# Two kv heads per 2 MB tile, on even and odd partitions, in a KV-cache decode layer

## Chip, cores and metric

The kernel runs on one core of a Trainium2 chip. The metric is the device time of one execution in microseconds (us). The median of the kernel before was 404.53 us over four runs (404.59 us over the three known when the prediction was made).

## The reference

It is one decode step of a layer with 4 sequences. Attention with 32 query heads and 16 kv heads looks at the last 4096 positions of a cache; then comes a gated feed-forward block.

```python
q = (layernorm(x) @ wq)                       # 4 x 32 heads x 128
k = k_cache[:, :, Sk - 4096:, :]              # 4 x 16 x 4096 x 128, bf16; V alike
p = softmax(einsum(q, k) * 128 ** -0.5)       # two query heads share a kv head
h = x + einsum(p, v) @ wo
g, u = layernorm(h) @ W_gate, layernorm(h) @ W_up      # 576 x 4608 each
out = h + (relu(g) * u) @ W_down
```

K and V of the window are 64 + 64 blocks of 1 MB (134.2 MB), and all weights together are 25.4 MB. Every byte is read once. The window of one head is 1 MB of contiguous memory; two neighbouring heads lie 4 MB apart.

## The kernel before

One DMA brings the 1 MB of one head and batch: partition p gets positions 32p to 32p+31, a contiguous run of 8 KB. K is transposed on TensorE (PE) in 32 blocks of 128 positions, copied from PSUM to SBUF, and multiplied with q. The scores of all 16 heads of a batch collect in two PSUM banks. P is then exponentiated, transposed, and multiplied with V. The sync engine (SP) issues all large loads in one order into a ring of 16 slots; it waits until the last reader of a slot is done.

```python
NSLOT = 16                     # slots of TILE = 4096 bf16 per partition = 1 MB
def add_kv(kind, i):
    b, kvh = divmod(i, KVH)
    s = ring_slot()
    off = slot0 + s * TILE
    src = (A_k_cache if kind == "K" else A_v_cache)[b, kvh, SK - WIN:SK, :].rearrange("(p t) d -> p (t d)", p=128)
    place((kind, i), off, TILE, ("TR", i) if kind == "K" else ("PV", i),
          lambda e: e.dma_start(out=arena[:, off:off + TILE], in_=src), key=f"slot{s}")
# ... (cut)
# QK: one head per tile, 512 neighbouring columns
    bank[4 + u][32 * j:32 * j + 32, :], lhsT=qTm[:, b, kvh, :],
    rhs=k[:, j * 1024 + u * 512:j * 1024 + (u + 1) * 512],
# exp of a batch, 1024 columns; then eight transposes of P and two copies into pTm
    act(("EXP", b), lambda e: e.activation(out=p_sb[:, :], in_=s_ps, func=ACT.Exp, ..., accum_out=stat[:, b, 2:3]), ...)
```

## Time and profile before

| quantity | value | where it is read |
|---|---|---|
| time | 404.5 us | median of the runs |
| DMA rate while K and V stream | 419 GB/s | windows of the profile |
| PE, DVE, ACT busy over the span | 66, 30, 34% | part 1 of the page |
| a K tile from issue to landing | 27.9 us | part 6 of the page |
| last W_down landed, end of span | 398.3, 402.3 us | chain of waits |

The first fence is from the page of the kernel before. In part 2 each column is a fortieth of the span: the digit is the busy share in tenths, then follow the GB/s moved. Part 6 gives the size of a DMA and the median time from issue to landing.

```profile
span 402.3 us, 10840 instructions
...
PE 265.4 (66%) x5091; PEld 209.7 (52%) x5091; DVE 121.9 (30%) x218; ACT 138.3 (34%) x154; POOL 3.9 (1%) x21
...
DMA  8999999999999999999999999999999999999992
GB/s 321 372 402 422 419 419 419 419 418 421 419 418 421 419 420 419 421 419 418 419 420 419 420 419 420 416 421 419 421 419 419 412 367 370 425 422 415 209 360 118
DMA packets 25172, 160.29 MB, mean 398 GB/s; under 512 B 2404, under 2 KB 6504, under 8 KB 6504
...
sb_arena<-in_A_k_cache_dram SPq DMA_DIRECT2D x64, 1024.0 KB, 27.9
```

The DMA engines are busy in every slice, and from slice 4 to slice 31 the rate hardly moves. A tile that needs 2.5 us of transfer lands 28 us after it was issued, so a long queue stands in front of the engines; 27.9 us at 419 GB/s is 11.7 MB. No compute engine is full. The kernel is bound by bytes per second of the DMA engines.

The second fence is the window view of the same kernel: start and end in us, length, busy us of PE, PE weight loads, DVE, ACT and POOL with instruction counts, granted clock, DMA share, GB/s.

```profile
87.00:200.00 113.00, 84.03 (x1637) 69.27 (x1636) 37.08 (x63) 45.89 (x49) 0.00 (x0) 0.86 1.01 419
200.00:320.00 120.00, 84.50 (x1777) 69.39 (x1776) 35.27 (x64) 42.59 (x47) 0.00 (x0) 0.81 1.01 419
```

The third is the end of its chain of waits (start us, us, what): the chain runs into the last W_down transfer, then 4 us of work.

```profile
335.17 18.48 DMA sb_arena<-in_A_v_cache_dram
...
359.93 38.40 DMA sb_arena<-in_B_W_down_dram
398.33 0.04 issue
398.38 1.30 PE psb L593 x32
```

The groups that the change touches in its arithmetic are the exp (L416), one of the two copies of the transposed P (L437), and QK (L402). They are four, four and 512 instructions (busy us, mean ns).

```profile
L402 PE MATMUL psb<-sb_arena,sb_qTm 128*32 128x512 bf16 x512 | 44.0, 425 | 1.0 <-ACT sb_p_sb L416 1.0
L437 DVE COPY sb_pTm<-psb 128x512 bf16<-128x512 bf16 x4 | 2.4, 593 | 3.6 <-PE psb L425 3.6
L416 ACT ACTIVATE sb_p_sb<-psb,sb_stat 128x1024 bf16<-128x1024 f32 x4 | 4.5, 1114 | 6.2 <-DVE sb_stat L412 6.2
```

### The profile page before, as it was taken

What the parts mean: (1) busy time and instruction counts of PE and PEld (TensorE: products, weight loads), DVE (VectorE), ACT (ScalarE), POOL (GpSimd) and SP (SyncE); (2) the same over time, 40 slices, a digit from 0 to 9 for tenths busy, and PEclk for the clock granted to TensorE, in tenths of its full rate; (3) what the DMA queues carried; (4) which work ended last, traced back from release to release, by engine and by line L of the source; (5) the groups of instructions that cost most, each with busy time, mean ns of one, the idle gap of its engine ahead of it and who ended that gap; (6) DMA issues with size and microseconds to landing.
All of it is one profiled execution on the core that took longest, in us unless ns stands there. A gap on an engine that the chain in (4) does not pass through costs nothing.

```text
span 402.3 us, 10840 instructions
## 1 busy us (share of the span) xinstructions
PE 265.4 (66%) x5091; PEld 209.7 (52%) x5091; DVE 121.9 (30%) x218; ACT 138.3 (34%) x154; POOL 3.9 (1%) x21
## 2 busy tenths in 40 slices
PE   4555999988777776867776767877774420465253
PEld 4244777766566655656564656666653320342022
DVE  4147555643222243422222433322232000011020
ACT  4222777754333353434333532533330100000010
POOL 3000000000000000000000000000000000000000
PEclk9866999999888889888889897988886555566556
DMA  8999999999999999999999999999999999999992
GB/s 321 372 402 422 419 419 419 419 418 421 419 418 421 419 420 419 421 419 418 419 420 419 420 419 420 416 421 419 421 419 419 412 367 370 425 422 415 209 360 118
DMA packets 25172, 160.29 MB, mean 398 GB/s; under 512 B 2404, under 2 KB 6504, under 8 KB 6504
## 3 DMA queue, kind: packets, MB, share of 16 engines
q1 hardware_dynamic: 25104, 159.59, 98.2%
q8 instruction: 40, 0.66, 0.7%
q10 hardware_dynamic: 24, 0.01, 0.0%
q14 instruction: 4, 0.03, 0.0%
HBM read 159.58 MB, written 0.00 MB: 397 GB/s over the span
## 4 chain that ended last, share of the span: by engine, by line
DMA 67%; PE 19%; SPq 9%; DVE 3%; issue 1%; ACT 0%
DMA sb_arena<-in_A_k_cache_dram 42%; PE psb L373 13%; DMA sb_arena<-in_A_v_cache_dram 11%; DMA sb_arena<-in_B_W_down_dram 10%; SPq L225 8%; DMA sb_arena<-in_A_wq_dram 4%; PE psb L402 3%; DVE sb_pTm L496 2%; PE psb L452 1%; PE psb L518 1%; SPq L232 1%; PE psb L593 0%; DVE sb_stat L410 0%; ACT sb_p_sb L416 0%; PE psb L331 0%
## 5 line engine op out<-in xcount | busy, mean ns | idle before, releaser
L373 PE MATMUL psb<-sb_ident_b,sb_arena 128*128 128x128 bf16 x2048 | 151.9, 243 | 60.4 <-DMA sb_arena<-in_A_k_cache_dram 53.8
L373 PEld LDWEIGHTS psb<-sb_ident_b,sb_arena 128*128 128x128 bf16 x2048 | 140.1, 111 | 74.2 <-DMA sb_arena<-in_A_k_cache_dram 60.2
L387 ACT COPY sb_arena<-psb 128x1024 bf16<-128x1024 bf16 x128 | 125.4, 1014 | 143.2 <-PE psb L373 143.2
L385 DVE COPY sb_arena<-psb 128x1024 bf16<-128x1024 bf16 x128 | 87.9, 690 | 152.0 <-PE psb L373 151.7
L452 PE MATMUL psb<-sb_arena,sb_pTm 128*32 128x128 bf16 x2048 | 49.2, 251 | 32.7 <-DMA sb_arena<-in_A_v_cache_dram 31.5
L452 PEld LDWEIGHTS psb<-sb_arena,sb_pTm 128*32 128x32 bf16 x2048 | 41.6, 113 | 50.7 <-DMA sb_arena<-in_A_v_cache_dram 35.5
L402 PE MATMUL psb<-sb_arena,sb_qTm 128*32 128x512 bf16 x512 | 44.0, 425 | 1.0 <-ACT sb_p_sb L416 1.0
L560 PE MATMUL psb<-sb_arena,sb_hnT 128*32 128x384 bf16 (+1 forms) x120 | 10.2, 500 | 14.8 <-DMA sb_arena<-in_B_W_up_dram 8.4
L523 ACT COPY sb_pTm<-psb 128x288 f32<-128x288 f32 x1 | 0.4, 398 | 46.4 <-PE psb L518 46.4
L478 DVE COPY sb_o_sb<-psb 128x128 f32<-128x128 f32 x4 | 1.2, 291 | 45.2 <-PE psb L452 45.2
L560 PEld LDWEIGHTS psb<-sb_arena,sb_hnT 128*32 128x32 bf16 (+1 forms) x120 | 4.0, 130 | 20.4 <-DMA sb_arena<-in_B_W_up_dram 10.4
L402 PEld LDWEIGHTS psb<-sb_arena,sb_qTm 128*32 128x32 bf16 x512 | 8.1, 97 | 9.0 <-issue 3.3
L564 ACT ACTIVATE sb_pTm<-psb 128x384 f32<-128x384 f32 x3 | 1.3, 492 | 23.9 <-PE psb L560 23.9
L567 DVE TENSOR_TENSOR sb_pTm<-psb,sb_pTm 128x384 bf16<-128x384 f32 x3 | 1.5, 550 | 24.0 <-ACT sb_pTm L564 24.0
L331 PE MATMUL psb<-sb_arena,sb_xnT 128*32 128x512 bf16 (+1 forms) x40 | 3.9, 478 | 6.8 <-DMA sb_arena<-in_A_wq_dram 6.4
L496 DVE MEMSET sb_pTm<- 128x8192 uint32 x1 | 6.9, 6885 | 1.6 <-issue 1.6
L593 PE MATMUL psb<-sb_arena,sb_pTm 128*32 128x144 bf16 x144 | 3.9, 277 | 4.2 <-DMA sb_arena<-in_B_W_down_dram 4.2
L416 ACT ACTIVATE sb_p_sb<-psb,sb_stat 128x1024 bf16<-128x1024 f32 x4 | 4.5, 1114 | 6.2 <-DVE sb_stat L412 6.2
L410 DVE TENSOR_REDUCE sb_stat<-psb 128x1 f32<-128x1024 f32 x4 | 4.9, 1225 | 4.3 <-PE psb L402 4.3
L468 ACT ACTIVATE sb_stat<-sb_stat 128x1 f32<-128x1 f32 x4 | 0.8, 203 | 14.5 <-DVE sb_stat L466 14.5
L593 PEld LDWEIGHTS psb<-sb_arena,sb_pTm 128*32 128x32 bf16 x144 | 3.2, 121 | 4.8 <-DMA sb_arena<-in_B_W_down_dram 4.6
L331 PEld LDWEIGHTS psb<-sb_arena,sb_xnT 128*32 128x32 bf16 (+1 forms) x40 | 0.7, 99 | 9.2 <-DMA sb_arena<-in_A_wq_dram 8.7
(94 smaller groups left out, 64.7 us busy)
## 6 DMA issues: line engine op xcount, KB each, us to landing
sb_arena<-in_A_k_cache_dram SPq DMA_DIRECT2D x64, 1024.0 KB, 27.9
sb_arena<-in_A_v_cache_dram SPq DMA_DIRECT2D x64, 1024.0 KB, 27.6
sb_arena<-in_B_W_down_dram SPq DMA_DIRECT2D x4, 1296.0 KB, 36.5
sb_arena<-in_A_wo_dram SPq DMA_DIRECT2D x1, 4608.0 KB, 31.7
sb_arena<-in_B_W_gate_dram SPq DMA_DIRECT2D x4, 1152.0 KB, 27.0
sb_arena<-in_B_W_up_dram SPq DMA_DIRECT2D x4, 1152.0 KB, 28.4
sb_arena<-in_A_wq_dram SPq DMA_DIRECT2D x4, 1024.0 KB, 11.2
sb_arena<-in_B_W_gate_dram SPq DMA_DIRECT2D x1, 576.0 KB, 33.5
```

What stands on the lines that cost most here:

```text
L225: lambda e: e.dma_start(out=arena[:, off:off + TILE], in_=src), key=f"slot{s}")
L331: pe("QMM", lambda e, c=c, w=w, off=off, n=n, g=g, bk=bk: e.matmul(bank[4 + bk][32 * g:32 * g + 32, :], lhsT=xnT[0:w, c, :], rhs=arena[0:w ...
L373: o = pe(("TRJ", i, j), lambda e, j=j, u=u, t=t: e.transpose(out=bankb[TRB[j]][:, u * 128:(u + 1) * 128], in_=kn[:, t, :], identity=ident_ ...
L385: dve(("EV", i, j), lambda e: e.tensor_copy(out=dst, in_=src), deps)
L387: act(("EV", i, j), lambda e: e.copy(out=dst, in_=src), deps)
L402: o = pe(("QK", i), lambda e, u=u, j=j: e.matmul(bank[4 + u][32 * j:32 * j + 32, :], lhsT=qTm[:, b, kvh, :], rhs=k[:, j * 1024 + u * 512:j ...
L410: dve(("MAX", b), lambda e: e.tensor_reduce(out=stat[:, b, 0:1], in_=s_ps, axis=AX.X, op=ALU.max, negate=True), [("QK", b * KVH + KVH - 1)])
L416: act(("EXP", b), lambda e: e.activation(out=p_sb[:, :], in_=s_ps, func=ACT.Exp, bias=stat[:, b, 1:2], scale=SCALE, accum_out=stat[:, b, 2 ...
L452: pe(("PV", i), lambda e, tl=tl, j=j: e.matmul(o_ps[32 * j:32 * j + 32, 0:DH], lhsT=pTm[:, tl, j, kvh, :], rhs=v[:, 8 * j + tl, :], start= ...
L496: dve("c_pTm", lambda e: e.memset(pflat, 0.0))
L560: pe(("GU", c), lambda e, c=c, w=w, g=g, m=m, j=j, lo=lo: e.matmul(bank[3 * g + m][32 * j:32 * j + 32, 0:384], lhsT=hnT[0:w, c, :], rhs=ar ...
L593: pe("DOWN", lambda e, j=j, r=r, n=n, wv=wv: e.matmul(bank[0][32 * n:32 * n + 32, 0:144], lhsT=hhT[:, r * 128 + 32 * j:r * 128 + 32 * j + 32],
```

## The change

Its intent: longer contiguous runs per DMA packet. A run of 16 KB per partition means that 64 partitions hold a whole head, so a 128-partition tile holds two heads. Head 0 goes to the even partitions and head 1 to the odd ones, so that the source can be written with its 64 rows outermost (64 rows x 2 heads x 16 KB). The transposed K then has the two heads in alternate columns, and QK reads every second column. For PV both heads lie in the contraction: each column of P is written twice, transposed, and masked so that one head's weights are zero on odd partitions, the other's on even ones. The sum of exp counts each value twice, so it is multiplied by 0.5. Tiles are 2 MB in a ring of 8 slots. The wq rows are also brought in pairs, 16 KB per partition.

```diff
-NSLOT = 16
-TILE = 4096
-VDMA_LAG = KVH + 2
+NSLOT = 8
+TILE = 8192
+VDMA_LAG = BT + 1
@@ add_kv @@
-            src = (A_k_cache if kind == "K" else A_v_cache)[b, kvh, SK - WIN:SK, :].rearrange("(p t) d -> p (t d)", p=128)
+            src = cache[b, 2 * k2:2 * k2 + 2, SK - WIN:SK, :].rearrange("a (p t) d -> p a (t d)", p=64)
@@ pe_qk @@
-                        rhs=k[:, j * 1024 + u * 512:j * 1024 + (u + 1) * 512],
+                        bank[4 + u][32 * j:32 * j + 32, :], lhsT=qTm[:, b, 2 * k2 + a, :], rhs=k[:, j, :, :, a],
@@ act_exp @@
-            act(("EXP", b), lambda e: e.activation(out=p_sb[:, :], in_=s_ps, func=ACT.Exp, ...
+            act(("EXP", b), lambda e: e.activation(out=p_sb[:, :].rearrange("p (k a) -> p k a", a=2),
+                                                   in_=bass.AP(tensor=psb, offset=4 * 512, ap=[[4096, 128], [1, 1024], [0, 2]]), ...
@@ put_pT, now twice per batch @@
-                    dve(("PM", b, 0), lambda e, dst=dst, src=src: e.tensor_copy(out=dst, in_=src), deps)
+                dve(("PM", b, r, a), lambda e, dst=dst, src=src, a=a: e.tensor_scalar(
+                    out=dst, in0=src, scalar1=par[:, a:a + 1], scalar2=None, op0=ALU.mult), deps)
... (cut: ring bookkeeping, wq in pairs of rows, constants for parity and 0.5; of the old copies only the first is shown)
```

More of the change, by code (lines that the diff above doesn't have):

```diff
@@ L21 @@
 NPAIR = B * KVH
+NTILE = NPAIR // 2
+BT = KVH // 2
 SCALE = DH ** -0.5
@@ L25 @@
 NKT = 3
-NSLOT = 16
-TILE = 4096
+NSLOT = 8
+TILE = 8192
+UNIT = 4096
 QLAG = 2
-VDMA_LAG = KVH + 2
+VDMA_LAG = BT + 1
 PV_LAG = KVH + 3
@@ L144, in bass_sequential_preLN__sliding_block_cached__glu_gated_reglu__decode_kernel @@
         pool = lambda name, fn, deps=(): P.op("gpsimd", name, fn, deps)
-        arena = sb("arena", [128, (NKT + NSLOT) * TILE], BF16)
-        pTm = sb("pTm", [128, 8, 4, KVH, 32], BF16)
+        arena = sb("arena", [128, NKT * UNIT + NSLOT * TILE], BF16)
+        pTm = sb("pTm", [128, 16, 4, BT, 32], BF16)
         ident_b = sb("ident_b", [128, 128], BF16)
@@ L151, in bass_sequential_preLN__sliding_block_cached__glu_gated_reglu__decode_kernel @@
         ones_f = sb("ones_f", [128, 128], FP32)
+        ones_h = sb("ones_h", [128, 128], FP32)
         ones_d = sb("ones_d", [128, 128], FP32)
@@ L163, in bass_sequential_preLN__sliding_block_cached__glu_gated_reglu__decode_kernel @@
         qTm = sb("qTm", [128, B, KVH, 32], BF16)
-        p_sb = sb("p_sb", [128, 1024], BF16)
+        p_sb = sb("p_sb", [128, 2048], BF16)
+        half = sb("half", [128, 64], FP32)
+        par = sb("par", [128, 2], FP32)
         stat = sb("stat", [128, B, 8], FP32)
@@ L182, in bass_sequential_preLN__sliding_block_cached__glu_gated_reglu__decode_kernel @@
         hhT = pflat[:, 4608:4608 + 1152]
-        kT = [arena[:, i * TILE:(i + 1) * TILE] for i in range(NKT)]
-        slot0 = NKT * TILE
+        kT = [arena[:, i * UNIT:(i + 1) * UNIT] for i in range(NKT)]
+        slot0 = NKT * UNIT
         psb = es.enter_context(nc.psum_tensor("psb", [128, 8, 512], FP32))
@@ L210, in place @@
             land[name] = off
-        ring = [(-DC - 2 * NPAIR) % NSLOT]
+        ring = [(-3 - 2 * NTILE) % NSLOT]
         def ring_slot():
@@ L219, in add_kv, with add_wq @@
         def add_kv(kind, i):
-            b, kvh = divmod(i, KVH)
+            b, k2 = divmod(i, BT)
             s = ring_slot()
             off = slot0 + s * TILE
-            src = (A_k_cache if kind == "K" else A_v_cache)[b, kvh, SK - WIN:SK, :].rearrange("(p t) d -> p (t d)", p=128)
-            place((kind, i), off, TILE, ("TR", i) if kind == "K" else ("PV", i),
+            cache = A_k_cache if kind == "K" else A_v_cache
+            src = cache[b, 2 * k2:2 * k2 + 2, SK - WIN:SK, :].rearrange("a (p t) d -> p a (t d)", p=64)
+            place((kind, i), off, TILE, ("TR", 2 * i + 1) if kind == "K" else ("PV", 2 * i + 1),
                   lambda e: e.dma_start(out=arena[:, off:off + TILE], in_=src), key=f"slot{s}")
-        def add_wq(c):
+        wq_off = []
+        def add_wq(m):
             s = ring_slot()
             off = slot0 + s * TILE
-            w = _dw(c)
-            place(("wq", c), off, TILE, "QMM",
-                  lambda e: e.dma_start(out=arena[0:w, off:off + H * DH], in_=A_wq[c * 128:c * 128 + w, :]), key=f"slot{s}")
-        P.dma("scalar", ("L", "x"), lambda e: e.dma_start(out=x_bf[:, :], in_=A_x.rearrange("b s d -> (b s) d")), "d_x")
-        for s in range(2):
-            add_kv("K", s)
-        for c in range(DC):
-            add_wq(c)
-        for s in range(2, NPAIR):
+            if m < 2:
+                wq_off.extend([off, off + H * DH])
+                src = A_wq[m * 256:(m + 1) * 256, :].rearrange("(p r) n -> p (r n)", r=2)
+                place(("wq", m), off, TILE, "QMM", lambda e: e.dma_start(out=arena[:, off:off + TILE], in_=src), key=f"slot{s}")
+            else:
+                wq_off.append(off)
+                place(("wq", m), off, TILE, "QMM",
+                      lambda e: e.dma_start(out=arena[0:64, off:off + H * DH], in_=A_wq[512:576, :]), key=f"slot{s}")
+        P.dma("scalar", ("L", "x"), lambda e: e.dma_start(out=x_bf[:, :], in_=A_x.rearrange("b s d -> (b s) d")), "d_x")
+        add_kv("K", 0)
+        for m in range(3):
+            add_wq(m)
+        for s in range(1, NTILE):
             add_kv("K", s)
@@ L243, in bass_sequential_preLN__sliding_block_cached__glu_gated_reglu__decode_kernel @@
         for i in range(NKT):
-            for blk in range(i * TILE // 64, (i + 1) * TILE // 64):
+            for blk in range(i * UNIT // 64, (i + 1) * UNIT // 64):
                 owner[blk] = "QKEND"
@@ L249, in bass_sequential_preLN__sliding_block_cached__glu_gated_reglu__decode_kernel @@
         WDJ = 9 * D
-        rest = list(range(NPAIR - VDMA_LAG, NPAIR))
+        rest = list(range(NTILE - VDMA_LAG, NTILE))
         for n, v in enumerate(rest):
             add_kv("V", v)
-            if n == len(rest) - 7:
+            if n == len(rest) - 4:
                 place(("wo",), WO_OFF, H * D, "WO",
@@ L273, in kv @@
         def kv(kind, i):
-            off = land[(kind, i)]
+            off = land[(kind, i // 2)]
             return arena[:, off:off + TILE].rearrange("p (t d) -> p t d", d=DH)
@@ L284, in bass_sequential_preLN__sliding_block_cached__glu_gated_reglu__decode_kernel @@
                                                 compare_op=ALU.not_equal, fill=1.0, base=0, channel_multiplier=1), ["c_idf0"])
+        pool("c_half0", lambda e: e.memset(half[:, :], 0.0))
+        pool("c_half", lambda e: e.affine_select(out=half[:, :], in_=half[:, :], pattern=[[-2, 64]], compare_op=ALU.not_equal,
+                                                 fill=1.0, base=0, channel_multiplier=1), ["c_half0"])
+        pool("c_onesh", lambda e: e.memset(ones_h[:, :], 0.5))
         pool("c_ones", lambda e: e.memset(ones_f[:, :], 1.0))
@@ L300, in bass_sequential_preLN__sliding_block_cached__glu_gated_reglu__decode_kernel @@
         dve("c_eps", lambda e: e.memset(eps_c[:, :], EPS))
+        dve("c_par0", lambda e: e.tensor_reduce(out=par[:, 0:1], in_=half[:, :], axis=AX.X, op=ALU.max), ["c_half"])
+        dve("c_par", lambda e: e.tensor_scalar(out=par[:, 1:2], in0=par[:, 0:1], scalar1=-1.0, scalar2=1.0,
+                                               op0=ALU.mult, op1=ALU.add), ["c_par0"])
         dve("c_qTm", lambda e: e.memset(qTm[:, :, :, :], 0.0))
@@ L315, in bass_sequential_preLN__sliding_block_cached__glu_gated_reglu__decode_kernel @@
         tpv = bankb[6]
+        xn_rows = lambda c: (xn_bf[0:B, 512:576] if c == 4 else
+                             xn_bf[0:B, c // 2 * 256:c // 2 * 256 + 256].rearrange("b (p r) -> b r p", r=2)[:, c % 2, :])
         def pe_q():
@@ L319, in pe_q @@
                 w = _dw(c)
-                pe(None, lambda e, c=c, w=w: e.transpose(out=tpv[0:w, c * 4:(c + 1) * 4], in_=xn_bf[0:B, c * 128:c * 128 + w],
+                pe(None, lambda e, c=c, w=w: e.transpose(out=tpv[0:w, c * 4:(c + 1) * 4], in_=xn_rows(c),
                                                          identity=ident_b[0:B, 0:B]), ["xn", "c_idb"] if c == 0 else [])
@@ L327, in pe_q @@
                 w = _dw(c)
-                off = land[("wq", c)]
+                off = wq_off[c]
                 for n in range(8):
@@ L333, in pe_q @@
                         start=(c == 0), stop=(c == DC - 1), skip_group_check=True),
-                        ([("L", "wq", c)] + (["xnT", "c_xnT"] if c == 0 else [])) if n == 0 else [])
+                        ([("L", "wq", c // 2)] + (["xnT", "c_xnT"] if c == 0 else [])) if n == 0 and c % 2 == 0 else [])
             for bk in range(2):
@@ L363, in pe_tr @@
                 for u in range(8):
-                    t = j * 8 + u
+                    t = j * 16 + i % 2 * 8 + u
                     deps = []
                     if u == 0:
-                        deps = [("L", "K", i)] if j == 0 else []
+                        deps = [("L", "K", i // 2)] if j == 0 else []
                         if i == 0:
@@ L389, in pe_qk @@
         def pe_qk(i):
-            b, kvh = divmod(i, KVH)
-            k = kT[i % NKT]
-            for u in range(2):
+            dp, u = divmod(i, 2)
+            b, k2 = divmod(dp, BT)
+            k = kT[i % NKT].rearrange("p (j t k a) -> p j t k a", j=4, t=8, a=2)
+            for a in range(2):
                 for j in range(4):
                     deps = []
-                    if u == 0:
+                    if a == 0:
                         deps.append(("EV", i, j))
-                    if j == 0 and kvh == 0:
+                    if j == 0 and k2 == 0:
                         if b == 0:
@@ L401, in pe_qk @@
                             deps += [("EXP", b - 1), ("MAX", b - 1)]
-                    o = pe(("QK", i), lambda e, u=u, j=j: e.matmul(
-                        bank[4 + u][32 * j:32 * j + 32, :], lhsT=qTm[:, b, kvh, :],
-                        rhs=k[:, j * 1024 + u * 512:j * 1024 + (u + 1) * 512],
-                        start=(kvh == 0), stop=(kvh == KVH - 1), skip_group_check=True), deps)
+                    o = pe(("QK", i), lambda e, a=a, j=j: e.matmul(
+                        bank[4 + u][32 * j:32 * j + 32, :], lhsT=qTm[:, b, 2 * k2 + a, :], rhs=k[:, j, :, :, a],
+                        start=(k2 == 0 and a == 0), stop=(k2 == BT - 1 and a == 1), skip_group_check=True), deps)
             if i == NPAIR - 1:
@@ L415, in act_exp, with pe_pt @@
         def act_exp(b):
-            act(("EXP", b), lambda e: e.activation(out=p_sb[:, :], in_=s_ps, func=ACT.Exp, bias=stat[:, b, 1:2], scale=SCALE,
+            act(("EXP", b), lambda e: e.activation(out=p_sb[:, :].rearrange("p (k a) -> p k a", a=2),
+                                                   in_=bass.AP(tensor=psb, offset=4 * 512, ap=[[4096, 128], [1, 1024], [0, 2]]), func=ACT.Exp, bias=stat[:, b, 1:2], scale=SCALE,
                                                    accum_out=stat[:, b, 2:3]),
-                [("NB", b), ("PT", b - 1) if b else ("QT", 7)])
-        def pe_pt(b):
+                [("NB", b), ("PT", b - 1, 1) if b else ("QT", 7)])
+        def pe_pt(b, r):
             for tl in range(8):
@@ L423, in pe_pt, with put_pT @@
                 if tl == 0:
-                    deps = [("EXP", b), ("ONORM", b - 1) if b else "qTm"]
-                pe(("PT", b), lambda e, tl=tl: e.transpose(out=mb_ps[:, tl * 128:(tl + 1) * 128],
-                                                           in_=p_sb[:, tl * 128:(tl + 1) * 128], identity=ident_b[:, :]), deps)
-        def put_pT(b):
-            for half in range(2):
-                dst = bass.AP(tensor=pTm, offset=half * 4 * 4 * KVH * 32,
-                              ap=[[8 * 4 * KVH * 32, 128], [KVH * 32, 16], [34, KVH], [1, 2]])
-                src = mb_ps[:, half * 512:(half + 1) * 512].rearrange("p (a k h) -> p a k h", k=KVH, h=2)
-                deps = [("PT", b), "c_pTm"]
+                    deps = [("PM", b, 0, 0), ("PM", b, 0, 1)] if r else [("EXP", b), ("ONORM", b - 1) if b else "qTm"]
+                pe(("PT", b, r), lambda e, tl=tl: e.transpose(out=mb_ps[:, tl * 128:(tl + 1) * 128],
+                                                              in_=p_sb[:, (r * 8 + tl) * 128:(r * 8 + tl + 1) * 128],
+                                                              identity=ident_b[:, :]), deps)
+        def put_pT(b, r):
+            for a in range(2):
+                dst = bass.AP(tensor=pTm, offset=r * 8192 + 2 * a, ap=[[16384, 128], [256, 32], [36, BT], [1, 2]])
+                src = mb_ps[:, :].rearrange("p (m q a h) -> p m q a h", q=BT, a=2, h=2)[:, :, :, a, :]
+                deps = [("PT", b, r), "c_pTm", "c_par"]
                 if b:
                     deps.append(("PV", b * KVH - 1))
-                if half == 0:
-                    dve(("PM", b, 0), lambda e, dst=dst, src=src: e.tensor_copy(out=dst, in_=src), deps)
-                else:
-                    dve(("PM", b, 1), lambda e, dst=dst, src=src: e.tensor_copy(out=dst, in_=src), deps)
+                dve(("PM", b, r, a), lambda e, dst=dst, src=src, a=a: e.tensor_scalar(
+                    out=dst, in0=src, scalar1=par[:, a:a + 1], scalar2=None, op0=ALU.mult), deps)
         def pe_pv(i):
-            b, kvh = divmod(i, KVH)
+            dp, u = divmod(i, 2)
+            b, k2 = divmod(dp, BT)
             v = kv("V", i)
@@ L447, in pe_pv @@
                     if tl == 0 and j == 0:
-                        deps.append(("L", "V", i))
-                        if kvh == 0:
-                            deps += [("PM", b, 0), ("PM", b, 1)]
+                        deps.append(("L", "V", dp))
+                        if k2 == 0 and u == 0:
+                            deps += [("PM", b, r, a) for r in range(2) for a in range(2)]
                             deps.append(("OEV", b - 1) if b else "xT")
                     pe(("PV", i), lambda e, tl=tl, j=j: e.matmul(
-                        o_ps[32 * j:32 * j + 32, 0:DH], lhsT=pTm[:, tl, j, kvh, :], rhs=v[:, 8 * j + tl, :],
-                        start=(kvh == 0 and tl == 0), stop=(kvh == KVH - 1 and tl == 7), skip_group_check=True), deps)
+                        o_ps[32 * j:32 * j + 32, 0:DH], lhsT=pTm[:, u * 8 + tl, j, k2, :], rhs=v[:, 16 * j + 8 * u + tl, :],
+                        start=(k2 == 0 and u == 0 and tl == 0), stop=(k2 == BT - 1 and u == 1 and tl == 7),
+                        skip_group_check=True), deps)
         def weights(b):
             pe(("MT", b), lambda e: e.matmul(m_ps[0:1, 0:128], lhsT=stat[:, b, 0:1], rhs=ident_f[:, :], start=True, stop=True),
-               [("MAX", b), ("PM", b, 0), ("PM", b, 1), "c_idf"])
+               [("MAX", b), ("PM", b, 1, 0), ("PM", b, 1, 1), "c_idf"])
             dve(("GM", b), lambda e: e.tensor_reduce(out=gm4[0:1, 0:32], in_=m_ps[0:1, 0:128].rearrange("p (j h) -> p h j", j=4),
@@ L472, in weights @@
                                                        scalar2=stat[:, b, 2:3], op0=ALU.mult, op1=ALU.mult), [("EXP", b)])
-            pe(("LS", b), lambda e: e.matmul(m_ps[:, 0:32], lhsT=ones_f[:, :], rhs=selw[:, 1, :], start=True, stop=True),
-               [("SELL", b)])
+            pe(("LS", b), lambda e: e.matmul(m_ps[:, 0:32], lhsT=ones_h[:, :], rhs=selw[:, 1, :], start=True, stop=True),
+               [("SELL", b), "c_onesh"])
             dve(("RL", b), lambda e: e.reciprocal(out=rL[:, :], in_=m_ps[:, 0:32]), [("LS", b)])
@@ L485, in bass_sequential_preLN__sliding_block_cached__glu_gated_reglu__decode_kernel @@
             if s >= PV_LAG and (s - PV_LAG) % KVH == 0:
-                pe_pt((s - PV_LAG) // KVH)
-                put_pT((s - PV_LAG) // KVH)
+                pe_pt((s - PV_LAG) // KVH, 0)
+                put_pT((s - PV_LAG) // KVH, 0)
             if s < NPAIR:
@@ L491, in bass_sequential_preLN__sliding_block_cached__glu_gated_reglu__decode_kernel @@
                     evac(s, j)
+            if s >= PV_LAG and (s - PV_LAG) % KVH == 0:
+                pe_pt((s - PV_LAG) // KVH, 1)
+                put_pT((s - PV_LAG) // KVH, 1)
             if s == 1:
```

## The prediction

> **What bounds it now.** The DMA queue. In the page's slices the DMA engines are 90% busy or more from about 10 to 390 us; windows give 419 GB/s from 87 to 320 us, with PE busy about 70%, DVE and ACT 30 to 40%. The sync engine's waits are for K slots to come free (66 us on the transposes), yet a K or V tile lands 28 us after its issue: about 11 MB are always queued, so compute lateness of some 20 us costs nothing. The chain of waits ends in the last W_down transfer (landed at 398.3 us) and 4 us of compute. Only bytes per second count; 160 MB stay.
>
> **What a packet costs.** The trace's packet records (commonest value, undisturbed): 1152 B 51 ns, 8192 B 309, 9216 B 347, 10368 B 389: 27.2 B/ns per engine plus about 8 ns. Sixteen times 27.2 is 435 GB/s, the ceiling in the Trainium skill, "DMA: Bandwidth & Descriptors", Where 436 GB/s comes from; the trace agrees. Each tile adds a 10 ns semaphore write per engine, and the mean 8 KB packet takes 314, not 309 ns.
>
> **What the change does to it.** K and V: 16,384 packets of 8 KB become 8,192 of 16 KB, 128 DMAs become 64; wq likewise. Estimate for 16 KB: 602 + 8 ns, plus 3 to 6 of the scatter: 613 to 616 ns. Per 2 MB and engine 8 x 615 + 10 = 4.93 us, against 2 x 2.50 = 5.00 us now: 426 GB/s (424 to 429). For 134 MB: 320.3 -> 315.0 us, 5.3 us saved (3.8 to 7.5), all on the critical path. wq saves 0.2 us. Unchanged: the start, wo in 1152 B packets (370 GB/s), the 64-partition remainders, W_down, the last 4 us.
>
> **What it adds, off the path.** Per batch: exp writes 2048 columns (1.11 -> about 2.1 us), eight more transposes (0.55 us), four masked DVE copies of about 0.6 us instead of two: 3 us x 4 batches, under 28 us of queued transfers. QK reads K with stride 2; if that doubled its 0.55 us per tile, PE would still keep up, with a thinner margin between 35 and 87 us, where PE sets the pace. Slots freed in 2 MB steps leave 12 to 14 MB in flight.
>
> **Predicted:** 404.6 - 5.4 = 399.2 us, 8 in 10 between 396.6 and 403.5. Faster by over 2% 0.09, within 2% 0.79, slower 0.12.
>
> **What would show it.** Steady GB/s 424 to 429; 16 KB packets of 610 to 616 ns; W_down landing about 5 us earlier; PE and ACT busy slightly up with no idle DMA slices; first transposes 2 us later without effect.
>
> **What would make it wrong.** (1) Ports. In 64-partition transfers packets take about 716 instead of 352 ns: two engines share a port (the skill, "SBUF — State Buffer", Door 1: partitions 0 to 63 reach half of the 16 ports). The source's slowest dimension is now 64 against 128 partitions. If each engine then gets eight neighbouring partitions instead of one port's set, pairs of engines meet on a port, packets grow towards 1200 ns, and the kernel takes 500 to 700 us. That is most of "slower". (2) The two heads lie 4 MB apart; if such alternating reads collide in HBM, packets grow. (3) The scatter may be per byte (less gain) or per packet (more). (4) The 14 us at 223 GB/s around the gate/up remainder may shift by 1 or 2 us.

## The result

The changed kernel took 398.56 us (398.44 to 398.88, four runs) against 404.53 us: ratio 0.9855, 95% interval 0.9838 to 0.9873. Ratios here are the mean time of one kernel's fast runs over the mean of the other's in the same rounds, so they are not quite the ratio of the medians quoted. Executions over 1.5% slower than the fastest of the same kernel are left out of the means. A second series, below, gave 0.9863. The gain is real but lies under the 2% line.

The page of the changed kernel, same parts as before:

```profile
span 396.6 us, 10818 instructions
...
PE 259.7 (65%) x5123; PEld 206.2 (52%) x5123; DVE 126.7 (32%) x228; ACT 141.3 (36%) x154; POOL 4.4 (1%) x24
...
DMA  7999999999999999999999999999999999999993
GB/s 313 385 406 426 418 425 431 422 428 423 423 430 423 425 425 430 430 421 425 425 430 423 425 430 425 429 423 425 423 430 430 410 369 368 426 424 419 229 354 142
DMA packets 15668, 160.28 MB, mean 404 GB/s; under 512 B 1348, under 2 KB 5448, under 8 KB 5448
...
sb_arena<-in_A_k_cache_dram SPq DMA_DIRECT2D x32, 2048.0 KB, 32.6
```

The windows, the end of the chain, and the groups of its arithmetic (L427 is QK, L462 the masked copies, L440 the exp):

```profile
87.00:200.00 113.00, 82.92 (x1681) 68.88 (x1674) 38.47 (x68) 47.05 (x50) 0.00 (x0) 0.86 1.01 426
200.00:320.00 120.00, 83.78 (x1829) 68.81 (x1826) 38.11 (x69) 44.31 (x47) 0.00 (x0) 0.83 1.01 424
```

```profile
329.14 19.90 DMA sb_arena<-in_A_v_cache_dram
...
356.87 35.79 DMA sb_arena<-in_B_W_down_dram
392.67 0.04 issue
392.71 1.30 PE psb L622 x27
```

```profile
L427 PE MATMUL psb<-sb_arena,sb_qTm 128*32 128x512 bf16 x512 | 44.5, 426 | 1.8 <-ACT sb_p_sb L440 1.8
...
L462 DVE TENSOR_SCALAR sb_pTm<-psb,sb_par 128x512 bf16<-128x512 bf16 x16 | 9.0, 639 | 6.0 <-PE psb L450 6.0
L440 ACT ACTIVATE sb_p_sb<-psb,sb_stat 128x2048 bf16<-128x2048 f32 x4 | 7.9, 1967 | 5.8 <-DVE sb_stat L436 5.8
```

The same bytes move in 9,504 fewer packets (8,448 fewer for K, V and wq, and 1,056 fewer 4-byte semaphore writes), at 424 to 426 instead of 419 GB/s, and the engines stay full. The last V tile landed at 349.0 us instead of 353.7 (18.48 and 19.90 us added to the starts shown), and W_down at 392.7 instead of 398.3. Between the first K/V packet and the last, the packet records of the two traces give 351.4 us before and 346.4 us after: 5.0 us of the gain. About 1 us more came in the stretch after the last V tile, whose code did not change (by the packet records 43.6 instead of 44.7 us); more on that stretch below. The exp, the copies and the transposes grew, and QK did not: reading every second column cost PE 426 against 425 ns.

### The profile page after: what moved, and what is told of

Same layout as the page of the kernel before. It is cut to its first block, busy times and chain, and to the rows that moved or that the text cites. A ratio compares the mean times of both kernels' runs of the same rounds, so it can differ in the third digit from the quotient of the medians.

```text
span 396.6 us, 10818 instructions
## 1 busy us (share of the span) xinstructions
PE 259.7 (65%) x5123; PEld 206.2 (52%) x5123; DVE 126.7 (32%) x228; ACT 141.3 (36%) x154; POOL 4.4 (1%) x24
## 4 chain that ended last, share of the span: by engine, by line
DMA 61%; PE 25%; SPq 6%; DVE 5%; issue 1%; ACT 1%
DMA sb_arena<-in_A_k_cache_dram 34%; PE psb L397 15%; DMA sb_arena<-in_A_v_cache_dram 13%; DMA sb_arena<-in_B_W_down_dram 9%; SPq L233 6%; DMA sb_arena<-in_A_wq_dram 5%; PE psb L427 4%; PE psb L477 3%; DVE sb_pTm L525 2%; DVE sb_pTm L462 1%; PE psb L547 1%; PE psb L450 1%; ACT sb_p_sb L440 1%; DVE sb_arena L409 0%; PE psb L622 0%
## 5 line engine op out<-in xcount | busy, mean ns | idle before, releaser
L397 PE MATMUL psb<-sb_ident_b,sb_arena 128*128 128x128 bf16 x2048 | 146.7, 238 | 58.3 <-DMA sb_arena<-in_A_k_cache_dram 54.8
L397 PEld LDWEIGHTS psb<-sb_ident_b,sb_arena 128*128 128x128 bf16 x2048 | 134.9, 108 | 71.8 <-DMA sb_arena<-in_A_k_cache_dram 58.0
L477 PE MATMUL psb<-sb_arena,sb_pTm 128*32 128x128 bf16 x2048 | 46.5, 246 | 36.7 <-DMA sb_arena<-in_A_v_cache_dram 32.5
L477 PEld LDWEIGHTS psb<-sb_arena,sb_pTm 128*32 128x32 bf16 x2048 | 40.5, 111 | 53.8 <-DMA sb_arena<-in_A_v_cache_dram 36.1
L427 PE MATMUL psb<-sb_arena,sb_qTm 128*32 128x512 bf16 x512 | 44.5, 426 | 1.8 <-ACT sb_p_sb L440 1.8
L589 PE MATMUL psb<-sb_arena,sb_hnT 128*32 128x384 bf16 (+1 forms) x120 | 8.7, 437 | 13.9 <-DMA sb_arena<-in_B_W_up_dram 7.3
L427 PEld LDWEIGHTS psb<-sb_arena,sb_qTm 128*32 128x32 bf16 x512 | 8.0, 96 | 9.5 <-issue 4.1
L462 DVE TENSOR_SCALAR sb_pTm<-psb,sb_par 128x512 bf16<-128x512 bf16 x16 | 9.0, 639 | 6.0 <-PE psb L450 6.0
L440 ACT ACTIVATE sb_p_sb<-psb,sb_stat 128x2048 bf16<-128x2048 f32 x4 | 7.9, 1967 | 5.8 <-DVE sb_stat L436 5.8
L450 PE MATMUL psb<-sb_ident_b,sb_p_sb 128*128 128x128 bf16 x64 | 5.7, 242 | 2.5 <-DVE sb_oT L507 1.3
L450 PEld LDWEIGHTS psb<-sb_ident_b,sb_p_sb 128*128 128x128 bf16 x64 | 4.4, 108 | 3.5 <-DVE sb_pTm L462 1.5
## 6 DMA issues: line engine op xcount, KB each, us to landing
sb_arena<-in_A_k_cache_dram SPq DMA_DIRECT2D x32, 2048.0 KB, 32.6
```

Source lines behind the costliest of these rows:

```text
L397: o = pe(("TRJ", i, j), lambda e, j=j, u=u, t=t: e.transpose(out=bankb[TRB[j]][:, u * 128:(u + 1) * 128], in_=kn[:, t, :], identity=ident_ ...
L427: o = pe(("QK", i), lambda e, a=a, j=j: e.matmul(bank[4 + u][32 * j:32 * j + 32, :], lhsT=qTm[:, b, 2 * k2 + a, :], rhs=k[:, j, :, :, a], ...
L440: act(("EXP", b), lambda e: e.activation(out=p_sb[:, :].rearrange("p (k a) -> p k a", a=2), in_=bass.AP(tensor=psb, offset=4 * 512, ap=[[4 ...
L450: pe(("PT", b, r), lambda e, tl=tl: e.transpose(out=mb_ps[:, tl * 128:(tl + 1) * 128], in_=p_sb[:, (r * 8 + tl) * 128:(r * 8 + tl + 1) * 128],
L462: dve(("PM", b, r, a), lambda e, dst=dst, src=src, a=a: e.tensor_scalar(out=dst, in0=src, scalar1=par[:, a:a + 1], scalar2=None, op0=ALU.m ...
L477: pe(("PV", i), lambda e, tl=tl, j=j: e.matmul(o_ps[32 * j:32 * j + 32, 0:DH], lhsT=pTm[:, u * 8 + tl, j, k2, :], rhs=v[:, 16 * j + 8 * u ...
```

## The experiments

Theory A says that each packet has a fixed time, and that halving the number of K and V packets is the gain. Rival B says that the gain comes from fewer and larger DMAs and a deeper queue. A third question is whether the added arithmetic takes something back. All kernels of one series ran on one chip beside the kernel before.

One caution on results: the attention output is tiny beside x with these inputs (computed from the reference, about 0.00005 against 0.05), so a kernel that mixes up heads still passes the comparison with the reference. Four kernels below are wrong. For the changed kernel and for the version with spread remainders, a functional simulation off the chip with enlarged inputs was made as well: there they agree with the reference as closely as the kernel before, and the heads-outermost kernel plainly does not. It was repeated, with K, V and wq enlarged 20 times and wo 40 times: the kernel before, the changed kernel, the one with 1 MB DMAs and the one with spread remainders all differ from the reference by 0.3%, the heads-outermost kernel by 68%.

### Control: the changed kernel again

No edit.

> Control: the changed kernel again, on the chip of the next three. Ratio to before 0.985 to 0.987 (about 398.5 us), steady 425 GB/s, 16 KB packets of 617 ns on average. Every comparison of this call is made against this.

Measured: 398.61 us (398.13 to 398.84), ratio 0.9863 (0.9849 to 0.9877), 426 GB/s in the window from 87 to 200 us, 16 KB packets of 616.7 ns on average between 90 and 320 us. As expected. Its window:

```profile
87.00:200.00 113.00, 83.72 (x1705) 69.52 (x1702) 39.74 (x70) 48.26 (x51) 0.00 (x0) 0.87 1.01 426
```

### 2 MB DMAs, 8 KB runs

The kernel before, with each DMA bringing two heads side by side in the free dimension. Only the loads and slots change.

```diff
-            src = (...)[b, kvh, SK - WIN:SK, :].rearrange("(p t) d -> p (t d)", p=128)
+            src = (...)[b, 2 * k2:2 * k2 + 2, SK - WIN:SK, :].rearrange("a (p t) d -> p a (t d)", p=128)
-                  lambda e: e.dma_start(out=arena[:, off:off + TILE], in_=src), ...
+                  lambda e: e.dma_start(out=arena[:, off:off + TILE].rearrange("p (a n) -> p a n", a=2), in_=src), ...
... (cut: ring of 8 slots, two wq loads to a slot, waits by tile of two heads)
```

> The kernel before with one change: each DMA brings two heads (2 MB, ring of 8 slots), but still in 8 KB runs, so 16,384 packets and 64 K/V DMAs; the arithmetic is untouched. Theory A (the gain is the fixed time of a packet): only the 10 ns semaphore writes of 64 DMAs go, 0.6 us; 403.5 to 404.5 us, 419 to 420 GB/s, 8 KB packets of 314 ns. Rival B (fewer, larger DMAs or the deeper queue are the gain): 398 to 400 us, as the changed kernel.

Measured: 403.93 us (403.39 to 405.45), ratio 1.0004 (0.9987 to 1.0022); 8 KB packets of 314.7 ns. The window of this run, and its K loads:

```profile
87.00:200.00 113.00, 80.19 (x1603) 66.16 (x1604) 35.70 (x61) 44.78 (x48) 0.00 (x0) 0.84 1.01 420
...
sb_arena<-in_A_k_cache_dram SPq DMA_DIRECT2D x32, 2048.0 KB, 32.8
```

Half as many DMAs, tiles of 2 MB and the ring of 8 slots are worth nothing that can be measured. Rival B falls.

### 1 MB DMAs, 16 KB runs

The changed kernel, each tile cut in two DMAs of one head on every second partition.

```diff
-                  lambda e: e.dma_start(out=arena[:, off:off + TILE], in_=src), key=f"slot{s}")
+            place(..., lambda e: e.dma_start(out=arena[0:128:2, off:off + TILE], in_=srcs[0]), key=f"slot{s}")
+            P.dma("sync", ..., lambda e: e.dma_start(out=arena[1:128:2, off:off + TILE], in_=srcs[1]), f"slotb{s}", [])
... (cut: the two sources, waits for both DMAs)
```

> The changed kernel with each 2 MB DMA cut in two of 1 MB, one head each, on every second partition: 16 KB runs and 8,192 packets stay, K/V DMAs are 128 again. Theory A: 0.6 us for the 64 more semaphore writes, about 399.2 us (398.5 to 400). Rival B: back to 403 or 404 us. If packets come out near 1,200 ns instead of 617, engines share ports in this pattern, and the run says so instead.

Measured: 398.62 us (397.9 to 400.02), ratio 0.9869 (0.985 to 0.9889), packets of 616.2 ns.

```profile
87.00:200.00 113.00, 83.03 (x1697) 68.47 (x1695) 39.37 (x69) 48.12 (x51) 0.00 (x0) 0.86 1.01 426
...
sb_arena<-in_A_k_cache_dram SPq DMA_DIRECT2D x64, 1024.0 KB, 30.4
```

With as many DMAs as the kernel before, but 16 KB packets, all of the gain is there. From the first K/V packet to the last, the packet records give 351.7 us in the previous run and 346.2 us in this one (351.4 before the change, 346.4 after it). These 5 us of the gain follow the run length, not the size or number of the DMAs. The placement of rows is not the cause either: the commonest 16 KB packet takes the same 611 ns here, with the heads outermost and in the 4 MB tiles below. The 1 us after the last K/V packet is another matter: that stretch takes 44.7 us before, 43.6 us changed, but 44.0 us also with 2 MB DMAs and 8 KB runs (one profile each), so the run length is not shown to be its cause. Nor is theory A's 0.6 us for the semaphore writes seen: 346.2 us with 128 DMAs against 346.4 with 64, and 351.4 against 351.7.

### 32 KB runs in 4 MB tiles

The changed kernel, with four heads interleaved; the arithmetic is left alone, so the result is wrong.

```diff
-NSLOT = 8
-TILE = 8192
+NSLOT = 4
+TILE = 16384
-            src = cache[b, 2 * k2:2 * k2 + 2, SK - WIN:SK, :].rearrange("a (p t) d -> p a (t d)", p=64)
+            src = cache[b, 4 * k4:4 * k4 + 4, SK - WIN:SK, :].rearrange("a (p t) d -> p a (t d)", p=32)
... (cut: slot bookkeeping, V loads issued 5 tiles after K, two wq loads to a slot, waits by tile of four heads)
```

> Wrong result on purpose (the arithmetic still takes two heads to a tile): the changed kernel with four heads in a 4 MB tile, 32 KB runs, 4,096 packets, ring of 4 slots. Theory A with the measured excess of a packet over 27.2 B/ns (617 - 602 = 14 ns, of which 5.7 scatter, hardly different from 8 KB, where it is 13 ns): 32 KB packets of about 1,219 ns, 256 packets fewer per engine, 3.7 us saved: 394.9 us (394 to 396.5), 430 GB/s. Rival D (the scatter is per byte): about 2 us saved, 396.5. If four slots are too few, DMA slices fall below 9 and it is slower than 398.5.

Measured: 411.36 us (408.94 to 417.0), of which the 417.0 is slow; the five fast runs have a median of 410.8 us (408.94 to 412.72), ratio 1.0166 (1.0137 to 1.0194). The expected gain did not come, and the expectation's last sentence did. The windows of this run (columns: span of time, its length, PE busy, granted clock, DMA share, GB/s):

```profile
30.00:40.00 10.00, 3.97 (x42) 0.67 0.50 213
40.00:50.00 10.00, 10.00 (x147) 0.87 0.63 251
50.00:60.00 10.00, 6.47 (x84) 0.83 1.00 431
60.00:100.00 40.00, 33.19 (x533) 0.92 1.00 430
```

Between 30 and 50 us the DMA engines are idle for a third to a half of the time. By the code, only four slots exist, wq holds two of them, and a slot comes free only when all four heads in it are used up. Where the queue is fed, the rate is 430 GB/s. Two things changed at once here, so a control was needed.

### 16 KB runs in the same 4 MB tiles

The kernel of the previous run with one number changed (also wrong).

```diff
-            src = cache[b, 4 * k4:4 * k4 + 4, SK - WIN:SK, :].rearrange("a (p t) d -> p a (t d)", p=32)
+            src = cache[b, 4 * k4:4 * k4 + 4, SK - WIN:SK, :].rearrange("a (p t) d -> p a (t d)", p=64)
```

> Wrong result on purpose (heads are paired differently than the arithmetic assumes): the kernel of e6_32k, 4 MB tiles in a ring of 4 slots, but with 16 KB runs (8,192 packets). e6_32k left two causes mixed. If the ring of 4 slots made it slow and 32 KB runs by themselves are a gain: the same idle DMA stretches between 30 and 50 us, and 2 to 4 us slower than e6_32k, 413 to 415.5 us. If 32 KB runs were themselves the loss: about 399 us here. Wherever the queue is fed (60 to 100 us): 425 GB/s here against 430 there.

Measured: 413.52 us (413.25 to 415.65), ratio 1.0244 (1.0221 to 1.0267).

```profile
30.00:40.00 10.00, 3.34 (x42) 0.67 0.47 200
40.00:50.00 10.00, 10.00 (x134) 0.78 0.60 239
50.00:60.00 10.00, 8.65 (x142) 1.00 1.01 433
60.00:100.00 40.00, 30.01 (x492) 0.91 1.00 425
```

The same idle stretch, and 425 against 430 GB/s where the queue is fed. So the ring of four 4 MB slots, with the order of loads that comes with it, costs about 15 us (413.5 against 398.6), and 32 KB runs by themselves give about 3 us back (fast runs: 413.5 against 410.8). Some 10 of the 15 us are lost between 30 and 50 us, worked out from the rates; later the ring falls short too, with 408 to 413 GB/s from 100 to 300 us against 426 in the changed kernel. Longer runs still pay where the queue is fed. The slots fill 128 KB of each partition already; a ring with more 4 MB slots was not tried.

### The added arithmetic once more

The changed kernel with exp, the second round of transposes, and all masked copies done twice.

```diff
+            act(("EXP2", b), lambda e: e.activation(... as EXP ...), [("EXP", b)])
-            for tl in range(8):
+            for tl in list(range(8)) * 2:
+                for n in range(2):      # around the masked copy
... (cut: what waited for EXP waits for EXP2)
```

> The changed kernel with the arithmetic that the change added done once more: exp of 2048 columns twice per batch (2.0 us ACT), the second eight transposes of P twice (0.6 us PE), each masked copy twice (2.5 us DVE). If it is hidden under the queued transfers: 398.3 to 399.2 us. If the added arithmetic costs time on the path, up to 5 us more per batch, 400 to 415 us.

Measured: 398.63 us (398.44 to 399.35), ratio 0.9867 (0.9852 to 0.9882).

```profile
PE 264.2 (67%) x5187; PEld 209.8 (53%) x5187; DVE 137.1 (35%) x244; ACT 149.0 (38%) x162; POOL 4.4 (1%) x24
```

ACT busy went from 141 to 149 us and DVE from 127 to 137 us, and the time did not move. The added arithmetic is off the path; nothing of the gain is taken back.

### Heads outermost in the source

The natural order of the dimensions. Its output is wrong, which doesn't matter for the time.

```diff
-            src = cache[...].rearrange("a (p t) d -> p a (t d)", p=64)
+            src = cache[...].rearrange("a (p t) d -> a p (t d)", p=64)
```

> Wrong result on purpose: the changed kernel with the source's dimensions in the natural order, heads outermost (2 x 64 rows of 16 KB). If the number of DMA engines follows the slowest dimension, only 2 of 16 work for K and V: 54 GB/s, about 2,500 us, K/V packets still about 611 ns. If it does not matter: 398.5 us.

Measured once: 2608.35 us. From its page:

```profile
GB/s 108 54 54 54 54 54 54 54 54 54 54 54 54 54 54 54 54 54 54 54 54 54 54 54 54 54 54 54 54 54 54 54 54 54 54 54 110 66 124 158
```

54 GB/s is two engines at 27 GB/s (16,384 B in 611 ns), and single packets most often take those 611 ns, as before. The Trainium skill, "DMA: Bandwidth & Descriptors", Why a DMA increments its semaphore by 16 and not by 1, says that the number of engines is the largest number up to 16 that divides the slowest dimension of both sides. With 2 outermost that is 2, and with 64 against 128 it is 16; both runs agree.

### One head on each half of the partitions

The other obvious way to 16 KB runs: two DMAs per tile of 64 partitions each. Its output is wrong, which doesn't matter for the time.

```diff
+            place(..., lambda e: e.dma_start(out=arena[0:64, off:off + TILE], in_=srcs[0]), key=f"slot{s}")
+            P.dma("sync", ..., lambda e: e.dma_start(out=arena[64:128, off:off + TILE], in_=srcs[1]), f"slotb{s}", [])
... (cut: the old load, the two sources, waits for both DMAs)
```

> Wrong result on purpose: the changed kernel with two 1 MB DMAs per tile, one head on partitions 0 to 63, the other on 64 to 127 (the other obvious way to 16 KB runs). If a 64-partition block reaches half of the ports: packets of about 1,220 ns, about 215 GB/s, 700 us or so. If engines spread over both DMAs and so over all ports: between 398.5 and 450 us.

Measured once: 697.86 us; packets of about 1,200 ns on average between 90 and 320 us. From its page:

```profile
DMA  9999999999999999999999999999999999999994
GB/s 256 271 211 211 214 212 219 216 219 218 222 215 221 216 221 219 222 220 222 223 216 224 224 225 228 228 237 235 227 227 231 227 235 235 273 214 211 413 246 206
```

All engines are busy at half speed. The Trainium skill, "SBUF — State Buffer", Door 1: The DMA port swizzle, states that partitions 0 to 63 reach 8 of the 16 ports and 64 to 127 the other 8; the run agrees. Alternate partitions, as in the run with 1 MB DMAs, had as many partitions per DMA (64) and full speed, so it is which partitions are hit, not how many.

### The 64-row remainders over all partitions

576 is 4 x 128 + 64, so the last 64 rows of wq, gate and up are loaded onto 64 partitions. Windows of the changed kernel's first profile, from 350 us on (columns as in the 32 KB run):

```profile
350.00:360.00 10.00, 7.33 (x118) 0.66 1.01 423
360.00:370.00 10.00, 4.97 (x84) 0.83 1.04 368
370.00:380.00 10.00, 2.54 (x32) 0.52 0.99 218
380.00:384.00 4.00, 1.27 (x14) 0.50 1.00 416
384.00:388.00 4.00, 3.93 (x93) 0.57 1.03 435
388.00:392.00 4.00, 0.75 (x36) 0.86 0.50 206
```

About 14 us run at half rate there, though the two remainders are only 1.2 MB. The edit loads each remaining row as two half rows on two partitions, and uses the two copies of x or h with the same parity mask that the change brought for P. The result is right.

```diff
-                      lambda e, off=off, w=w, W=W, c=c: e.dma_start(out=arena[0:w, off:off + F], in_=W[c * 128:c * 128 + w, :]))
+                          lambda e, off=off, W=W: e.dma_start(out=arena[:, off:off + F // 2],
+                                                              in_=W[512:576, :].rearrange("p (h n) -> (p h) n", h=2)))
-                            ... lhsT=hnT[0:w, c, :], rhs=arena[0:w, lo:lo + 384],
+                            ... lhsT=hnT[0:w, c + (c == 4) * (j // 2), :], rhs=arena[0:w, lo:lo + 384],
... (cut: wq alike; column offsets of the half rows; x and h of these 64 columns doubled, masked with par)
```

> The changed kernel with the three 64-row remainders (wq, gate, up) loaded as half rows over all 128 partitions, used through the same parity masks; correct result. In the changed kernel some 13 us around the last gate/up remainder run at 217 GB/s with packets of about 710 instead of 347 ns. If this is two engines meeting on half of the ports: that stretch returns to 420 GB/s, packets of 4608 B take 177 ns, 5 to 8 us saved: 391 to 394 us. If the half rate has another cause (the queue running dry, HBM), little moves: 397 to 399 us.

Measured: 390.68 us (390.37 to 390.76), ratio 0.9666 (0.9652 to 0.9679) to the kernel before, a little better than the 391 to 394 expected. This version beats both.

```profile
350.00:360.00 10.00, 5.85 (x81) 0.67 1.01 422
360.00:370.00 10.00, 6.21 (x88) 0.67 1.01 419
370.00:380.00 10.00, 7.33 (x129) 0.50 1.02 430
380.00:384.00 4.00, 1.54 (x47) 0.50 0.54 224
```

The half-rate stretch is gone, the 4608 B packets take 178 ns, and of the gate, up and W_down packets only 4 take over 600 ns, against 278 in the changed kernel. By the packet records, the stretch after the last K/V packet shrank from 43.6 to 37.7 us, and that up to it from 346.4 to 344.6 us (the wq remainder). How 1.2 MB could hold up 14 us in the changed kernel is only partly shown: there are only 128 remainder packets of gate and up, so packets of whole gate, up and W_down tiles were slow as well (97 of W_down, most of them 700 to 790 ns). That would fit engines that write whole tiles being slowed by engines still in a remainder. The records do not name the engine of a packet, so this is not shown, and the exact order stays open.

## Why the prediction was right

- **What bounds the kernel.** The DMA rate, as predicted. Doubling the added arithmetic moved nothing (398.63 us).
- **The fixed time of a packet.** The commonest times of six packet sizes in the runs:

| bytes | ns | bytes / 27.2 | rest |
|---|---|---|---|
| 1,152 | 51 | 42.4 | 8.6 |
| 4,096 | 159 | 150.6 | 8.4 |
| 8,192 | 309 | 301.2 | 7.8 |
| 10,368 | 389 | 381.2 | 7.8 |
| 16,384 | 611 | 602.4 | 8.6 |
| 32,768 | 1,213 | 1,204.7 | 8.3 |

  The prediction's line, made from four sizes up to 10 KB, gave 610 ns for 16 KB and 1,213 for 32 KB. The Trainium skill, "DMA: Bandwidth & Descriptors", Where 436 GB/s comes from, gives a ceiling of 435 GB/s, and 16 x 27.2 is that number.
- **The scatter above it.** 314.4 - 309 = 5.4 ns at 8 KB and 616.7 - 611 = 5.7 ns at 16 KB: it did not grow with the bytes. The mean came out 0.7 ns above the predicted 613 to 616.
- **The sum.** Predicted 426 GB/s and 5.3 + 0.2 us. Measured 424 to 426 GB/s, and 5.0 us between the first and the last K/V packet. In wall time one engine takes 8,192 B in 312.8 ns at 419 GB/s (8,192 x 16 / 419), and 16,384 B in 615.4 ns at 426. Over 512 packet pairs per engine, (2 x 312.8 - 615.4) x 512 is 5.2 us. The close match is partly luck: the prediction set wall time before (2.50 us per MB) against a sum of packet times after. Packet times on both sides, (2 x 314.4 - 616.7) x 512, give 6.2 us, more than the 5.0 measured; the records show a DMA share of 1.01, so packets overlap a little and their times do not add up exactly. Of the 6.0 us saved in all (forecast 5.4), about 1 us came after the last K/V packet and is no part of this sum.
- **The semaphore writes and the number of DMAs.** Predicted 10 ns each, 0.6 us in all. The two runs that vary the number of DMAs do not show it (stretches above); this term of the sum is not confirmed.
- **Off the path.** exp 1.97 us against the predicted 2.1; the masked copies 0.64 us as predicted 0.6; QK unslowed. The first transposes came at 8.5 instead of 5.8 us, without effect that shows. PE busy was forecast slightly up and fell from 265.4 to 259.7 us; why was not looked into. In flight: 32.6 us x 426 GB/s is 13.9 MB, in the predicted 12 to 14.
- **The ports.** The feared case did not come: 64 source rows against 128 partitions still give 616.7 ns packets. The halves run shows that the danger was of the right size (predicted 500 to 700 us, measured 698 us there). The two heads 4 MB apart, the second fear, did no harm that shows.
- **The tail.** The prediction allowed 1 or 2 us for the stretch at the gate/up remainder, and about 1 us came, on the good side. It also took the remainders as simply unchanged. They were, but they were worth 7.9 us, more than the whole change.

## What to carry to other kernels

When the DMA engines are full, count packets as well as bytes: fit the packet times of the trace to bytes and a constant, and the gain of a longer run can be worked out before anything is written. A longer run has to keep a multiple of 16 outermost on both sides, reach all partitions' ports, and leave enough slots in the ring; each of these, broken, cost far more than the 1.4% gained. A small transfer on 64 partitions in a full queue can cost about three times its own bytes (here 1.2 MB would need 2.8 us at 426 GB/s, and spreading it saved 5.9 us), so spread remainders over all partitions.

## What the Trainium skill lacked or had wrong

- "DMA: Bandwidth & Descriptors", Specifications, puts line rate at 512 B and more, and the page tells of a fixed overhead per packet where it explains small descriptors. Here about 8 ns per packet were still visible up to 32 KB: 419 GB/s with 8 KB runs, 426 with 16 KB, 430 with 32 KB where the queue was fed.
- "DMA: Bandwidth & Descriptors", Where 436 GB/s comes from, says that for HBM to SBUF the HBM side (about 358 GB/s) binds, although its own table has a 16 MB transfer at 425 and the note under that table keeps about 358 for the case that both cores of a pair stream. This single core drew 419 to 430 GB/s from HBM over hundreds of microseconds.
- "DMA: Bandwidth & Descriptors", The descriptor swizzle, describes a plain transfer to 128 partitions only. Two other shapes ran at full speed: 64 x 2 source rows onto 128 partitions (616.7 ns per 16 KB) and 64 rows onto every second partition (616.2 ns).
- "SBUF — State Buffer", Door 1, tells the rate of a 64-partition transfer by itself. No page says of loads from HBM how much it slows the stretch of the queue around it (the nearest is about back-pressure in remote DMA): about 14 us at 218 GB/s for 1.2 MB of gate and up remainders, and 5.9 us gained there when they were spread, 7.9 us with that of wq.
- No page relates the size of a tile to the depth of the ring that feeds the queue: the same 16 MB of slots gave 398.6 us as 8 x 2 MB and 413.5 us as 4 x 4 MB.
